# A single-token decode block on one core: every third cache pair of the main loop is loaded from ScalarE's queue instead of SyncE's

## The chip, the cores and the metric

The kernel runs on one core of one Trainium2 chip. The core's engines each follow their own instruction stream: TensorE (PE) multiplies matrices, VectorE (DVE) and ScalarE (ACT) work element by element, GpSimd (POOL) does little here, and SyncE (SP) mostly issues transfers. Transfers between the chip's memory (HBM) and the core's on-chip memory (SBUF) are carried out by 16 DMA engines; an engine that issues a transfer puts it on a queue of its own. Engines wait for each other through semaphores. The metric is the device time of one execution in microseconds (us), smaller is better.

## What is computed

Two batch rows of 512 numbers pass through a block: layer norm, attention of one new token against a cache of 8192 positions with 32 heads of 128, an output projection, a residual; then layer norm, a dense layer to 1792, squared ReLU, a dense layer back to 512, a residual. Cut to what matters:

```python
q = (layernorm(x) @ wq)                       # x: 2 x 512, wq: 512 x 4096
scores = einsum("bhqd,bhkd->bhqk", q, k_cache) * 128 ** -0.5   # k_cache: 2 x 32 x 8192 x 128
o = einsum("bhqk,bhkd->bhqd", softmax(scores), v_cache)        # v_cache: the same shape
h = x + o @ wo                                # wo: 4096 x 512
r = maximum(layernorm(h) @ w1 + b1, 0)        # w1: 512 x 1792
return h + (r * r) @ w2 + b2                  # w2: 1792 x 512
```

All of it is 32-bit floats. The two caches hold 2 x 268 MB, and each number of them is used once.

## The kernel before, in words

**The stream.** A "pair" is one head of one batch row; there are 64. The host lays out a pair's keys and values side by side, 128 partitions (rows of SBUF) by 16384 numbers, of which the first half is keys: 8,388,608 bytes, one row of 65,536 bytes per partition. One transfer brings a pair. SBUF has room for three pairs, the three slots of `ring` (line 191); pair i goes to slot i mod 3, and below u stands for that remainder.

**Before the loop** (lines 212 to 315) SP issues `wq` into slot 2, x, and pairs 0 and 1; the queries of all heads are computed; then pair 2 is issued into slot 2, in the place of `wq` (line 307).

**The loop** handles pairs 0 to 62, three to a round. For each pair PE waits for its data (`kv_full[u]`) and for a free score buffer, and multiplies the query with the keys: 32 matrix multiplications into score buffer S[k], k = u mod 2 (line 345). DVE takes the maximum (line 351), ACT the exponentials with their sum (line 358), DVE multiplies the values with the exponentials, four instructions with a sum each, writing over the values (line 363), and copies the pair's six sums away (line 367), which signals `kv_free`. SP runs a loop of its own (line 326): it takes `kv_free`, passes it on to PE as `s_free` (a score buffer is free), and issues the next pair into the slot. PE takes two `s_free` ahead of u = 0, none ahead of u = 1 and one ahead of u = 2. So u = 0 starts only when the pair ahead of it, which used the same score buffer S[0], is done; u = 1 and u = 2 may start their matrix multiplications while DVE still works on the pair ahead.

**Each engine's order.** In the loop the order of every engine is written out by hand. DVE does all of one pair before it touches the next. ACT does one exponential per pair in the same loop as PE and DVE (line 332). The code before and after the loop goes through the class `Line`, which records operations in order and adds the waits that their tiles need.

**After the loop** SP's order is (lines 479 to 495): take `kv_free` for pair 60 and issue the keys of pair 63 into slot 0; take `kv_free` for pair 61 and issue, into slot 1, the first half of `wo`, then 7/8 of the values of pair 63 (slot 0), then more of `wo`; take `kv_free` for pair 62 and issue the rest of `wo`, the rest of the values, `w1` and `w2` in six pieces. PE, in the meantime, takes one `s_free` (`token`, line 462), computes the scores of pair 63 (line 499), takes another, and the kernel joins the four sub-blocks of each pair, projects with `wo`, and runs the dense layers as the weights land. The last steps are the matrix multiplications with the last piece of `w2`, a copy and the transfer of the result (line 586).

Of the kernel before, what the change touches and what calls it, by code (L numbers as in the profile page):

```python
# [4 lines left out]
AF = mybir.ActivationFunctionType  # L5
ALU = mybir.AluOpType
AX = mybir.AxisListType
ENGINE = mybir.EngineType
# [12 lines left out]
SLOTS = 3  # L21
LOOPED = 63
# [151 lines left out]
def attention_block_kernel(nc, xd, kvd, wqd, wod, w1d, w2d, out):  # L174
    def sb(name, *shape):
        return nc.alloc_sbuf_tensor(name, [P, *shape], F32).ap()

    written = nc.alloc_semaphore("written")
    line = Line(nc)
    pe, dve, act, sp = nc.tensor, nc.vector, nc.scalar, nc.sync  # L180
    kv_full = [nc.alloc_semaphore(f"kv_full{u}") for u in range(SLOTS)]
    s_full, m_full, e_full, v_done, kv_free, s_free = (
        nc.alloc_semaphore(n) for n in ("s_full", "m_full", "e_full", "v_done", "kv_free", "s_free"))


    pick = sb("pick", NQ, P)
# [5 lines left out]
    def place(u):  # L192
        return ring[:, u * ROW : (u + 1) * ROW]

    def slot(i):
        return place(i % SLOTS)

    def keys(i):
        return slot(i)[:, :HALF].rearrange("p (j c) -> p j c", j=NQ)

    def values(i):
        return slot(i)[:, HALF:].rearrange("p (e c) -> p e c", e=NH)
# [13 lines left out]
        line.load(xr[at : at + B], xd)  # L216
    for i in range(2):
        line.op("sp", lambda e, i=i: e.dma_start(slot(i), kvd[i]).then_inc(kv_full[i], 16))
    line.op("sp", lambda e: e.sem_inc(s_free, 2))


    ones_d = sb("ones_d", P)
# [10 lines left out]
    S = [nc.alloc_psum_tensor(f"s{k}", [P, NQ * BLK], F32).ap() for k in range(2)]  # L233

    def banks(k):
        return [S[k][:, n * BLK : (n + 1) * BLK] for n in range(NQ)]
# [51 lines left out]
    for k in range(2):  # L288
        for d in range(DB):
            for j in range(NQ):  # L290
                n = k * NQ + j
# [11 lines left out]
    q3 = sb("q3", SLOTS, 32)  # L303
    QR = sb("QR", BH - LOOPED, 32)
# [6 lines left out]
    NM, LS, AC = ALL[:, :, 0], ALL[:, :, 1], ALL[:, :, 2:]  # L311
    st3 = sb("st3", SLOTS, ST)

    line.op("pe", lambda e: e.wait_ge(s_free, 2), [q3, QR], [S[0], S[1]])
    line.flush()

    def take(engine, sem, n=1):
        engine.wait_ge(sem, n).then_inc(sem, -n)  # L318

    def freed():  # L320

        take(sp, kv_free)
        sp.sem_inc(s_free, 1)

    kv3 = kvd[:LOOPED].rearrange("(r u) p c -> r u p c", u=SLOTS)
    with nc.Fori(1, LOOPED // SLOTS, 1, engines=[ENGINE.SP]) as r:
        for u in range(SLOTS):
            freed()
            sp.dma_start(slot(u), kv3[bass.ds(r, 1), u].rearrange("o p c -> p (o c)")).then_inc(kv_full[u], 16)
    all3 = ALL[:, :LOOPED].rearrange("p (r u) c -> p r u c", u=SLOTS)  # L330
    qt3 = QT[:, SLOTS : SLOTS + LOOPED].rearrange("p (r u) -> p r u", u=SLOTS)
    with nc.Fori(0, LOOPED // SLOTS, 1, engines=[ENGINE.PE, ENGINE.DVE, ENGINE.Activation],
                 head_slot={ENGINE.PE: 0}) as r:
        for u in range(SLOTS):
            k = u % 2
            s, bk = S[k], banks(k)

            if u == 0:
                take(pe, s_free, 2)
            if u == 2:  # L340
                take(pe, s_free)
            take(pe, kv_full[u], 16)
            for n in range(CS // BLK):
                for j in range(NQ):
                    made = pe.matmul(bk[n][32 * j : 32 * j + 32, :], q3[:, u, :], keys(u)[:, j, n * BLK : (n + 1) * BLK],  # L345
                                     start=True, stop=True)
            made.then_inc(s_full, 1)

            nm, ls = st3[:, u, 0:1], st3[:, u, 1:2]
            take(dve, s_full)  # L350
            dve.tensor_reduce(nm, s, axis=AX.X, op=ALU.max, negate=True).then_inc(m_full, 1)  # L351
            if u == SLOTS - 1:
                nxt = qt3[:, bass.ds(r, 1)].rearrange("p o c -> p (o c)")
                dve.tensor_scalar(q3, nxt[:, :, None].to_broadcast([P, SLOTS, 32]), 1.0, None,  # L354
                                  op0=ALU.mult)

            take(act, m_full)
            act.activation(s, s, AF.Exp, bias=nm, scale=1.0, accum_out=ls).then_inc(e_full, 1)  # L358

            take(dve, e_full)  # L360
            for e in range(NH):
                v = values(u)[:, e]
                made = dve.scalar_tensor_tensor(v, v, 1.0, s, op0=ALU.mult, op1=ALU.mult,  # L363
                                                accum_out=st3[:, u, 2 + e : 3 + e])
            made.then_inc(v_done, 1)
            take(dve, v_done)
            dve.tensor_scalar(all3[:, bass.ds(r, 1), u], st3[:, u : u + 1], 1.0, None,  # L367
                              op0=ALU.mult).then_inc(kv_free, 1)


    def scores(i, k):
        s, bk = S[k], banks(k)
        for n in range(CS // BLK):
            for j in range(NQ):
                line.matmul(bk[n][32 * j : 32 * j + 32, :], QR[:, i - LOOPED, :], keys(i)[:, j, n * BLK : (n + 1) * BLK])
# [22 lines left out]
    def weigh_max(n, pn):  # L398

        a, b = g_at[n]  # L400
        pn = pn[:, : NQ * (b - a)].rearrange("p (j i) -> p j i", j=NQ)
        for j in range(NQ):
            line.matmul(pn[:, j], pick[:, j, :], NM[:, a:b])
# [45 lines left out]
    def load_half(i, half):  # L449
        cut = slice(half * HALF, (half + 1) * HALF)  # L450
        line.load(slot(i)[:, cut], kvd[i][:, cut])
# [5 lines left out]
    def load_wo(a, b):  # L457

        cut = slice(a * D, b * D + (BIAS if b == H else 0))
        line.load(ring[:, ROW:][:, cut], wod[:, cut])  # L460

    def token():

        line.op("pe", lambda e: e.wait_ge(s_free, 1).then_inc(s_free, -1))  # L464

    def free():

        line.op("sp", lambda e: e.wait_ge(kv_free, 1).then_inc(kv_free, -1))
        line.op("sp", lambda e: e.sem_inc(s_free, 1))  # L469

    last = BH - 1
    bk0, bk1 = banks(0), banks(1)
    hp, sums, y, o = bk0
# [2 lines left out]
    gl = sb("gl", B)  # L476


    free()
    load_half(last, 0)  # L480
    free()
    load_wo(0, H // 2)
    load_values(0, 7 * CS // 2)
    load_wo(H // 2, H // 2 + WO_PIECES[0])
    free()
    load_wo(H // 2 + WO_PIECES[0], H)
    load_values(7 * CS // 2, CS // 2)
    at = 0
# [6 lines left out]
        at += n  # L495


    token()
    scores(last, 1)
    token()  # L500
    weigh_max(0, y)
    maximum(last, 1)
    exponentials(last, 1)
# [10 lines left out]
    y, o = y[:, :FQ], o[:, :P]  # L514
# [108 lines left out]
```

## Time and profile before

| what | value |
|---|---|
| median of 3 runs | 1301.19 us (1300.82 to 1301.35) |
| the profiled execution's own time | 1301.16 us |
| its span, first to last instruction | 1299.8 us |
| busy: PE, DVE, ACT | 422.4, 742.9, 143.7 us |
| moved by DMA | 561.16 MB, mean 432 GB/s |
| time of the packets of the one data queue, as a share of 16 engines' span | 99.7% |
| granted TensorE clock, mean | 0.634 |

The profile is one execution. Its page gives the busy time of each engine, the span in 40 slices, the DMA queues, the chain of work that ended last, the costliest groups of instructions and the DMA issues. Other views of the same trace give the instructions in order of time (the timeline: start, duration, engine, line, operation, output and input tile, count, and in brackets the idle time of the engine before it and what ended that), the waits added up by line, and the busy time in chosen stretches (the windows). "SPq" is SP's queue of DMA issues, "PEq" and the like an engine's own sequencer: "<-PEq L318" stands for a wait on a semaphore by the helper at line 318. "L345" is line 345 of the kernel. The time from issue to landing of a transfer includes its time behind others in the queue. 1 MB is a million bytes, while the KB in the page's list of issues is 1024 bytes.

### The profile page before, as it was taken

The numbers are of one execution on the slowest core, as the hardware profiler recorded it, in microseconds if no ns is written. First come the engines' busy times: TensorE is split into PE (matmuls) and PEld (weight loads), VectorE is DVE, ScalarE is ACT, GpSimd is POOL, SyncE is SP. The second block draws the span as 40 slices with busy tenths as digits, with TensorE's granted clock in tenths as the row PEclk, the third lists the DMA queues.
The fourth block names the chain that finished last, engine by engine and source line by source line (L and its number), as shares of the span: only waits on it lengthen the run. The fifth ranks groups of instructions, "written<-read, shape, count | busy, mean of one in ns | idle before, by whom it ended". The sixth has DMA issues, their size and how long they took to land. (4 is left out here: it accounts for less than half of the span.)

```text
span 1299.8 us, 6711 instructions
## 1 busy us (share of the span) xinstructions
PE 422.4 (32%) x2418; PEld 113.7 (9%) x2418; DVE 742.9 (57%) x709; ACT 143.7 (11%) x149; POOL 0.7 (0%) x6
## 2 busy tenths in 40 slices
PE   1423233223323323313313323322323332331347
PEld 0100000000000000000000000000000000000012
DVE  1355655655665564665665565665566565657474
ACT  1110010111011011011011011011101011101111
POOL 0000000000000000000000000000000000000000
PEclk9766566666566566656566556656656656666678
DMA  9999999999999999999999999999999999999998
GB/s 420 420 450 419 450 421 442 430 426 446 422 448 421 450 422 442 430 430 442 422 450 421 448 424 448 422 450 421 436 436 421 450 422 448 424 448 422 450 412 371
DMA packets 11069, 561.16 MB, mean 432 GB/s; under 512 B 1234, under 2 KB 1332, under 8 KB 1720
## 3 DMA queue, kind: packets, MB, share of 16 engines
q1 hardware_dynamic: 11064, 561.08, 99.7%
q8 instruction: 4, 0.07, 0.0%
q14 instruction: 1, 0.01, 0.0%
HBM read 561.03 MB, written 0.05 MB: 432 GB/s over the span
## 5 line engine op out<-in xcount | busy, mean ns | idle before, releaser
L345 PE MATMUL s<-ring,q 128*32 128x512 f32 x2016 | 376.1, 914 | 831.2 <-PEq L318 831.2
L363 DVE SCALAR_TENSOR_TENSOR ring<-ring,s 128x2048 f32<-128x2048 f32 x252 | 561.5, 2285 | 143.1 <-DVEq L318 143.1
L351 DVE TENSOR_REDUCE st<-s 128x1 f32<-128x2048 f32 x63 | 144.4, 2292 | 341.9 <-DVEq L318 341.9
L358 ACT ACTIVATE s<-s,st 128x2048 f32<-128x2048 f32 x63 | 122.3, 1942 | 1083.4 <-ACTq L318 1083.4
L345 PEld LDWEIGHTS s<-ring,q 128*32 128x32 f32 x2016 | 94.5, 159 | 1112.0 <-issue 1112.0
L363 DVE DVE_READ_ACCUMULATOR ring<-ring,s 128x1 f32 x252 | 21.0, 83 | 0.0
L367 DVE TENSOR_SCALAR ALL<-st 128x6 f32 x63 | 10.8, 172 | 15.2 <-DVEq L318 15.2
L165 DVE TENSOR_REDUCE sx<-xr 2x1 f32<-2x512 f32 x1 | 0.7, 676 | 21.2 <-DMA xr<-in_xd 21.2
L358 ACT ACTIVATION_READ_ACCUMULATOR s<-s,st 128x1 f32 x63 | 12.1, 193 | 0.0
L139 PE MATMUL s<-ring,OT 128*2 128x512 f32 (+1 forms) x70 | 10.8, 689 | 3.6 <-DMA ring<-in_wod 3.0
L139 PE MATMUL s<-ident,xr 128*128 128x4 f32 x8 | 1.9, 356 | 26.0 <-DVE xr L157 26.0
L139 PE MATMUL s<-ring,xn 128*2 128x512 f32 x64 | 9.2, 742 | 0.3 <-DVE xn L150 0.3
L161 DVE SCALAR_TENSOR_TENSOR ring<-ring,s 128x2048 f32<-128x2048 f32 x3 | 6.8, 2283 | 1.4 <-DMA ring<-in_kvd 1.4
L139 PE MATMUL s<-ring,QR 128*32 128x512 f32 x32 | 5.3, 825 | 4.6 <-DMA ring<-in_kvd 4.6
L157 DVE TENSOR_SCALAR QT<-s 128x64 f32<-128x64 f32 x1 | 0.2, 225 | 10.3 <-PE s L139 10.3
L139 PE MATMUL s<-ring,xc 128*2 128x448 f32 (+1 forms) x34 | 5.6, 725 | 0.3 <-DVE xc L153 0.3
L143 ACT ACT_TABLE_LOAD x4 | 5.1, 1283 | 0.8 <-PEq L615 0.7
L354 DVE TENSOR_SCALAR q<-QT 128x96 f32 x21 | 5.1, 243 | 0.0
L139 PE MATMUL s<-ALL,pick 128*128 128x62 f32 (+1 forms) x16 | 3.4, 352 | 5.1 <-PEq L464 4.5
L139 PE MATMUL s<-ring,a 128*2 128x128 f32 x112 | 3.6, 272 | 2.5 <-DMA ring<-in_w2d 1.8
L139 PEld LDWEIGHTS s<-ident,xr 128*128 128x128 f32 x8 | 1.8, 327 | 26.0 <-DVE xr L157 26.0
L150 DVE COPY res<-s 128x128 f32<-128x128 f32 x1 | 0.3, 292 | 5.9 <-PE s L139 5.9
(86 smaller groups left out, 50.9 us busy)
## 6 DMA issues: line engine op xcount, KB each, us to landing
ring<-in_kvd SPq DMA_DIRECT2D x1, 4096.0 KB, 28.3
ring<-in_wod SPq DMA_DIRECT2D x1, 4096.0 KB, 18.1
ring<-in_kvd SPq DMA_DIRECT2D x1, 3584.0 KB, 26.3
ring<-in_w1d SPq DMA_DIRECT2D x2, 1792.0 KB, 24.8
ring<-in_wod SPq DMA_DIRECT2D x1, 2560.0 KB, 31.8
ring<-in_w2d SPq DMA_DIRECT2D x2, 1280.0 KB, 30.5
ring<-in_wod SPq DMA_DIRECT2D x1, 1568.0 KB, 18.2
ring<-in_kvd SPq DMA_DIRECT2D x63, 37.3
```

What stands on the lines that cost most here:

```text
L139: self.op("pe", lambda e: e.matmul(out, lhsT, rhs, start=start, stop=stop), [lhsT, rhs], [out])
L143: self.op("act", lambda e: e.activation(out, in_, func, bias=bias, scale=scale, accum_out=accum_out), [in_, *more], [out] + ([] if accum_o ...
L150: self.op("dve", lambda e: e.tensor_copy(out, in_), [in_], [out])
L157: self.op("dve", lambda e: e.tensor_scalar(out, in_, by, None, op0=ALU.mult), [in_, *more], [out])
L161: self.op("dve", lambda e: e.scalar_tensor_tensor(out, a, by, b, op0=op0, op1=op1, accum_out=accum_out), [a, b, *more], [out] + ([] if acc ...
L165: self.op("dve", lambda e: e.tensor_reduce(out, in_, axis=AX.X, op=op, negate=negate), [in_], [out])
L345: made = pe.matmul(bk[n][32 * j : 32 * j + 32, :], q3[:, u, :], keys(u)[:, j, n * BLK : (n + 1) * BLK], start=True, stop=True)
L351: dve.tensor_reduce(nm, s, axis=AX.X, op=ALU.max, negate=True).then_inc(m_full, 1)
L354: dve.tensor_scalar(q3, nxt[:, :, None].to_broadcast([P, SLOTS, 32]), 1.0, None, op0=ALU.mult)
L358: act.activation(s, s, AF.Exp, bias=nm, scale=1.0, accum_out=ls).then_inc(e_full, 1)
L363: made = dve.scalar_tensor_tensor(v, v, 1.0, s, op0=ALU.mult, op1=ALU.mult, accum_out=st3[:, u, 2 + e : 3 + e])
L367: dve.tensor_scalar(all3[:, bass.ds(r, 1), u], st3[:, u : u + 1], 1.0, None, op0=ALU.mult).then_inc(kv_free, 1)
```

## The change

The loads of the loop's pairs with u = 1 (pairs 4, 7, ... 61, twenty transfers) are issued by ACT, on ACT's own DMA queue. SP's loop keeps u = 0 and u = 2. The two semaphores that carried the news of a free slot are split accordingly: the copy at the end of a pair with u = 1 signals `kv_free1`, which ACT takes and passes on to PE as `s_free1`. PE, which took two `s_free` ahead of u = 0, takes one `s_free` and one `s_free1` there.

ACT leaves the common loop and gets one of its own, so that its order can hold the load: exponentials of u = 0, exponentials of u = 1, the wait for the end of the pair u = 1 and the issue of its successor, exponentials of u = 2. Its loop has one round less than PE's and DVE's; the exponentials of the last round stand behind it. After the loop all transfers are still SP's, in the same order; the second `free` takes `kv_free1`, and the first `token` takes `s_free1`.

```diff
+    def next_load(engine, sem, freed, u, r):
+        take(engine, sem)
+        engine.sem_inc(freed, 1)
+        engine.dma_start(slot(u), kv3[bass.ds(r, 1), u].rearrange("o p c -> p (o c)")).then_inc(kv_full[u], 16)
+
+    def exponentials_of(u):
+        take(act, m_full)
+        act.activation(S[u % 2], S[u % 2], AF.Exp, bias=st3[:, u, 0:1], scale=1.0,
+                       accum_out=st3[:, u, 1:2]).then_inc(e_full, 1)
+
     with nc.Fori(1, LOOPED // SLOTS, 1, engines=[ENGINE.SP]) as r:
-        for u in range(SLOTS):
-            freed()
-            sp.dma_start(slot(u), kv3[bass.ds(r, 1), u].rearrange("o p c -> p (o c)")).then_inc(kv_full[u], 16)
+        for u in (0, 2):
+            next_load(sp, kv_free, s_free, u, r)
+    with nc.Fori(1, LOOPED // SLOTS, 1, engines=[ENGINE.Activation]) as r:
+        exponentials_of(0)
+        exponentials_of(1)
+        next_load(act, kv_free1, s_free1, 1, r)
+        exponentials_of(2)
+    for u in range(SLOTS):
+        exponentials_of(u)
...
-    with nc.Fori(0, LOOPED // SLOTS, 1, engines=[ENGINE.PE, ENGINE.DVE, ENGINE.Activation],
-                 head_slot={ENGINE.PE: 0}) as r:
+    with nc.Fori(0, LOOPED // SLOTS, 1, engines=[ENGINE.PE, ENGINE.DVE], head_slot={ENGINE.PE: 0}) as r:
...
             if u == 0:
-                take(pe, s_free, 2)
+                take(pe, s_free)
+                take(pe, s_free1)
...
-            take(act, m_full)
-            act.activation(s, s, AF.Exp, bias=nm, scale=1.0, accum_out=ls).then_inc(e_full, 1)
...
-                              op0=ALU.mult).then_inc(kv_free, 1)
+                              op0=ALU.mult).then_inc(kv_free1 if u == 1 else kv_free, 1)
...
-    free()
+    free(kv_free, s_free)
     load_half(last, 0)
-    free()
+    free(kv_free1, s_free1)
     load_wo(0, H // 2)
...
-    token()
+    token(s_free1)
     scores(last, 1)
-    token()
+    token(s_free)
```

More of the change, by code (lines that the diff above doesn't have):

```diff
@@ L181, in attention_block_kernel @@
     kv_full = [nc.alloc_semaphore(f"kv_full{u}") for u in range(SLOTS)]
-    s_full, m_full, e_full, v_done, kv_free, s_free = (
-        nc.alloc_semaphore(n) for n in ("s_full", "m_full", "e_full", "v_done", "kv_free", "s_free"))
+    s_full, m_full, e_full, v_done, kv_free, kv_free1, s_free, s_free1 = (
+        nc.alloc_semaphore(n)
+        for n in ("s_full", "m_full", "e_full", "v_done", "kv_free", "kv_free1", "s_free", "s_free1"))
     pick = sb("pick", NQ, P)
@@ L218, in attention_block_kernel @@
         line.op("sp", lambda e, i=i: e.dma_start(slot(i), kvd[i]).then_inc(kv_full[i], 16))
-    line.op("sp", lambda e: e.sem_inc(s_free, 2))
+    for sem in (s_free, s_free1):
+        line.op("sp", lambda e, sem=sem: e.sem_inc(sem, 1))
     ones_d = sb("ones_d", P)
@@ L312, in attention_block_kernel @@
     st3 = sb("st3", SLOTS, ST)
-    line.op("pe", lambda e: e.wait_ge(s_free, 2), [q3, QR], [S[0], S[1]])
+    line.op("pe", lambda e: e.wait_ge(s_free, 1), [q3, QR], [S[0], S[1]])
     line.flush()
@@ L318, in take @@
         engine.wait_ge(sem, n).then_inc(sem, -n)
-    def freed():
-        take(sp, kv_free)
-        sp.sem_inc(s_free, 1)
     kv3 = kvd[:LOOPED].rearrange("(r u) p c -> r u p c", u=SLOTS)
-    with nc.Fori(1, LOOPED // SLOTS, 1, engines=[ENGINE.SP]) as r:
-        for u in range(SLOTS):
-            freed()
-            sp.dma_start(slot(u), kv3[bass.ds(r, 1), u].rearrange("o p c -> p (o c)")).then_inc(kv_full[u], 16)
+    def next_load(engine, sem, freed, u, r):
[6 more added lines that the diff above has]
+                       accum_out=st3[:, u, 1:2]).then_inc(e_full, 1)
+    with nc.Fori(1, LOOPED // SLOTS, 1, engines=[ENGINE.SP]) as r:
+        for u in (0, 2):
[7 more added lines that the diff above has]
+        exponentials_of(u)
     all3 = ALL[:, :LOOPED].rearrange("p (r u) c -> p r u c", u=SLOTS)
     qt3 = QT[:, SLOTS : SLOTS + LOOPED].rearrange("p (r u) -> p r u", u=SLOTS)
-    with nc.Fori(0, LOOPED // SLOTS, 1, engines=[ENGINE.PE, ENGINE.DVE, ENGINE.Activation],
-                 head_slot={ENGINE.PE: 0}) as r:
+    with nc.Fori(0, LOOPED // SLOTS, 1, engines=[ENGINE.PE, ENGINE.DVE], head_slot={ENGINE.PE: 0}) as r:
         for u in range(SLOTS):
@@ L347, in attention_block_kernel @@
             made.then_inc(s_full, 1)
-            nm, ls = st3[:, u, 0:1], st3[:, u, 1:2]
+            nm = st3[:, u, 0:1]
             take(dve, s_full)
@@ L460, in load_wo, with token, free @@
         line.load(ring[:, ROW:][:, cut], wod[:, cut])
[L462 to L469, printed above, removed]
+    def token(sem):
+        line.op("pe", lambda e: e.wait_ge(sem, 1).then_inc(sem, -1))
+    def free(sem, freed):
+        line.op("sp", lambda e: e.wait_ge(sem, 1).then_inc(sem, -1))
+        line.op("sp", lambda e: e.sem_inc(freed, 1))
     last = BH - 1
@@ L484, in attention_block_kernel @@
     load_wo(H // 2, H // 2 + WO_PIECES[0])
-    free()
+    free(kv_free, s_free)
     load_wo(H // 2 + WO_PIECES[0], H)
```

## The prediction, made before the changed kernel was run

> **What bounds the kernel now.** I read the page's slices and queues first, then the windows, then the timeline around two boundaries between pairs.
>
> ```profile
> span 1299.8 us, 6711 instructions
> PE 422.4 (32%) x2418; PEld 113.7 (9%) x2418; DVE 742.9 (57%) x709; ACT 143.7 (11%) x149; POOL 0.7 (0%) x6
> DMA  9999999999999999999999999999999999999998
> q1 hardware_dynamic: 11064, 561.08, 99.7%
> ```
>
> No compute engine is busy for more than 57%, while the packets of the one queue fill 99.7% of the 16 DMA engines. The windows say whether there are gaps anywhere:
>
> ```profile
> core 0: us, PE busy (x) PEld busy (x) DVE busy (x) ACT busy (x) POOL busy (x), PEclk, DMA share, GB/s
> 62.00:1203.00 1141.00, 354.22 (x1888) 88.62 (x1888) 674.88 (x610) 121.46 (x118) 0.00 (x0) 0.61 1.00 434
> 1203.00:1243.00 40.00, 12.95 (x72) 3.41 (x76) 22.77 (x20) 4.12 (x4) 0.00 (x0) 0.63 1.01 436
> 1243.00:1261.00 18.00, 8.96 (x61) 2.13 (x53) 11.83 (x12) 2.06 (x2) 0.00 (x0) 0.87 1.01 434
> 1261.00:1297.00 36.00, 27.01 (x256) 12.07 (x260) 16.75 (x37) 7.32 (x14) 0.00 (x0) 0.81 0.96 408
> ```
>
> The DMA share is 1.00 through the whole loop and on to 1261 us, at 434 GB/s. So the kernel is a stream without holes: the time is the bytes over that rate, and it can only change if the rate does, or if the engines run dry somewhere. A pair is 8.389 MB, so at 434 GB/s its data takes 19.33 us and a round of three 58.0 us.
>
> How far is it from running dry? The cycle of a slot, in the middle of the loop:
>
> ```profile
> 604.09 6.28 PE L345 MATMUL s<-ring,q 128*32 128x512 f32 x32 [13.64 <-PEq L318]
> 604.40 0.17 DVE L367 TENSOR_SCALAR ALL<-st 128x6 f32 x1 [0.24 <-DVEq L318]
> 610.55 2.29 DVE L351 TENSOR_REDUCE st<-s 128x1 f32<-128x2048 f32 x1 [5.97 <-DVEq L318]
> 612.96 1.94 ACT L358 ACTIVATE s<-s,st 128x2048 f32<-128x2048 f32 x1 [17.86 <-ACTq L318]
> 624.32 0.17 DVE L367 TENSOR_SCALAR ALL<-st 128x6 f32 x1 [0.24 <-DVEq L318]
> 624.88 6.13 PE L345 MATMUL s<-ring,q 128*32 128x512 f32 x32 [14.51 <-PEq L318]
> ...
> 1164.32 6.06 PE L345 MATMUL s<-ring,q 128*32 128x512 f32 x32 [13.80 <-PEq L318]
> 1184.34 0.17 DVE L367 TENSOR_SCALAR ALL<-st 128x6 f32 x1 [0.24 <-DVEq L318]
> 1184.81 18.51 SPq L329 DMA_DIRECT2D ring<-in_kvd  x2
> ```
>
> A pair with u = 1 lands and PE starts at 1164.32; SP issues its successor at 1184.81, 20.5 us later. Where the scores are ready, a pair occupies DVE from the maximum at 610.55 to the end of its copy at 624.49, 13.94, say 14.0 us. What a transfer costs beside its data I take from the first one, which met an empty queue:
>
> ```profile
> ring<-in_wqd SPq DMA_DIRECT2D x1, 22.0
> DMA to landing us min/median/max: 35.4/37.2/39.6
> L329 SPq DMA_DIRECT2D ring<-in_kvd x60: 332/333/343, 62.0 to 1203.0; - x60
> ```
>
> 22.0 - 19.33 = 2.7 us, ahead of the first byte and behind the last together. So from the end of one pair's data to the first byte that its successor can bring into the slot pass 20.5 + 2.7 = 23.2 us. In the loop a transfer needs 37.2 us to land, and 37.2 - 22.0 = 15.2 of these it stands in line: the stream always has a spare. The spare is smallest behind the loop:
>
> ```profile
> 1222.30 6.09 PE L345 MATMUL s<-ring,q 128*32 128x512 f32 x32 [13.76 <-PEq L318]
> 1242.34 0.17 DVE L367 TENSOR_SCALAR ALL<-st 128x6 f32 x1 [0.24 <-DVEq L318]
> 1242.66 0.34 SPq L136 DMA_DIRECT2D ring<-in_wod  x1
> 1251.14 5.32 PE L139 MATMUL s<-ring,QR 128*32 128x512 f32 x32 [4.57 <-DMA ring<-in_kvd]
> 1260.71 2.29 DVE L165 TENSOR_REDUCE ALL<-s 128x1 f32<-128x2048 f32 x1
> 1260.85 0.33 SPq L136 DMA_DIRECT2D ring<-in_wod  x1
> ```
>
> Pair 61 lands at 1222.30, is done at 1242.5, and only then may `wo` be issued into its slot, at 1242.66. What is then still under way is pair 62 and the half pair of keys of 63, which lands at 1251.14. A transfer must be issued 2.7 us ahead of that landing to follow without a hole; it is issued 8.48 us ahead. The spare is 8.48 - 2.7 = **5.8 us**.
>
> **The change, part by part.** *The bytes, the three slots and the order of consumption* stay. *Issue:* 20 of SP's issues go to ACT. SP has nothing else to do in the loop: its 0.33 us each was hidden and saves nothing. On ACT an issue with its wait and its increment is not in this trace; from below it is nothing, from above I take SP's whole way from the start of the copy to the issue, 1184.34 to 1184.81, 0.5 us. What is queued behind it on ACT is the exponential of u = 2, whose maximum starts no sooner than that copy ends and comes 2.4 us ahead of the exponential (610.55, 612.96). 2.4 us cover 0.5, so I take 0; without cover it would be 20 x 0.5 = 10 us of compute, and of stream only as far as it exceeds a spare (below). ACT's wait for the end of pair u = 1 lasts while ACT has nothing to do in any case: the next maximum is behind that end on DVE. *PE* gets a second wait ahead of u = 0, for a semaphore that was set 14 us before: between 0 and the 0.24 us that a DVE wait shows at 624.32, only on compute that has a spare; 0. *ACT's own loop* has the same exponentials: 0.
>
> *The order of the bytes* is the real term. One queue served pairs strictly one after the other. With two queues that both hold work I let each engine alternate between them, half of the rate each. No row of this trace shows two busy data queues, so this is bounded: strict order as before (cost 0) and the halves that follow. I take the halves, as nothing in 16 independent engines keeps an order across queues.
>
> Count in data time within a round, 0 being the end of the data of u = 0, y that of u = 1, z that of u = 2, and 58.0 the next round's 0. The transfer of u = 1 (ACT) can start 23.2 after its predecessor's end, at y - 58 + 23.2 = y - 34.8. That of u = 2 (SP) starts 14.0 later, at y - 20.8, as DVE does u = 2 right behind u = 1. Until 0 the ACT transfer shares with u = 0 and gets (34.8 - y)/2; from 0 to y - 20.8 it is alone and gets y - 20.8; the rest of its 19.33 comes at half rate. So y = (y - 20.8) + 2 x (19.33 - (34.8 - y)/2 - (y - 20.8)), and y = 24.7. At that moment u = 2 has half of 24.7 - 3.9 = 20.8 us, **10.4 us of data**; it ends at z = 24.7 + 8.9 = 33.6, within the 14.0 that DVE needs anyway. Then u = 0 runs alone until the ACT transfer starts at 24.7 + 23.2 = 47.9, has 14.3 by then, shares the last 5.0 and ends at 58.0: it closes. The intervals between landings go from 19.3, 19.3, 19.3 to 24.7, 8.9, 24.4. The least that ever remains when a new transfer can start is those 5.0 us, so **no hole in the loop**: cost 0, uncovered if a load came over 5 us late.
>
> *Behind the loop* all is SP's, but pair 61 has paid for 62: when it lands, 10.4 us of 62 have been fetched that formerly came later. As the engines never rested, it lands 10.4 us later than before: PE starts it at 1232.7, and `wo` is issued at 1242.66 + 10.4 = 1253.1. The half pair still lands at 1251.1, because all that precedes it is the same bytes. The hole is 10.4 - 5.8 = **4.6 us**. Nothing wins it back: everything behind it up to the last piece of `w2` is stream. Pair 62 is done 14.0 us after 61, at 1266.9 instead of 1260.7, and releases the last pieces at 1267.1; by then the queue holds `wo`, values and `wo` of 4096 + 3584 + 2560 KB, 24.2 us from 1255.7 on, so there is a spare of 10. Compute at the end is 6.2 us late, 1.6 more than the stream, and has these waits for transfers to absorb it:
>
> ```profile
> 1269.33 2.29 DVE L161 SCALAR_TENSOR_TENSOR ring<-ring,s 128x2048 f32<-128x2048 f32 x1 [1.37 <-DMA ring<-in_kvd]
> 1294.97 1.27 PE L139 MATMUL s<-ring,a 128*2 128x128 f32 x40 [1.12 <-DMA ring<-in_w2d]
> 1296.88 1.06 PE L139 MATMUL s<-ring,a 128*2 128x128 f32 x32 [0.63 <-DMA ring<-in_w2d]
> ```
>
> 1.12 + 0.63 = 1.75 cover 1.6; without them 1.6 would be added. **Sum:** 1301.16 (the profiled execution's time) + 4.6 = 1305.8. The median, 1301.19, gives the same. A row is 65,536 bytes, 8 rows per engine and pair, 19.33/8 = 2.4 us each; if an engine alternates by whole rows, y, and with it the hole, may sit up to one such step off: about 2.2 to 7.0 us, 1303.4 to 1308.2 as this case's own range.
>
> **The rivals.** *Whole transfers in turn.* If an engine finishes its share of one transfer before it turns to the other queue, then at the end of u = 1 only u = 2 waits, and at the end of u = 2 only u = 0 (the ACT load can start 23.2 - 19.3 = 3.9 us later): the old order, no hole, 1301.2, no change; in effect the change would not do what it says. For it: 8 rows are a small share to finish. Against it: nothing in the rows. The Trainium skill, "DMA: Bandwidth & Descriptors", section "Queues, rings and completion order", says that an engine takes turns between queues by packets, typically of 9 to 17 descriptors; a share of 8 rows and its signal would be one such packet, and by that the time is 1301.2. The page of the profile counts rows as packets, 65,536 bytes at most, by which the turn comes after each row; no run so far shows which.
>
> *The rate falls while two queues are served.* The place is the shared time, 20.8 + 10.1 of each 58 us, 53% of the loop. The only slower rate of a busy stretch is that of small pieces, 408 GB/s at a share of 0.96, 425 when full, 2% under 434: 0.53 x 0.02 x 1141 = 12 us at most, so up to 1318; it decides from 0.4%, 2.6 us, on. Against it: in 1243 to 1261 pieces of unlike sizes follow each other at the full 434.
>
> *The rate rises.* If a second queue fills moments between rows, the share of 1.00 hides a reserve. The best window has 436, 0.5% over 434: 0.53 x 0.005 x 1141 = 3 us less. With the hole that is 1302.8; faster than before only if pair 61 also lands in the old order, 1298.2. Against it: 434 in every window of the loop. The Trainium skill, the same page, section "Issuing engines are not separate DMA queues", says that transfers from several engines run on the same 16 DMA engines and that this saves only issue time; by that this rival is excluded, and the trace agrees as far as one queue already fills 99.7%.
>
> *ACT's load comes late in the loop.* Above the 5.0 us spare each microsecond is a hole per round, 20 us in all. From ACT's 0.5 us that is far: 1306 to 1326.
>
> **How the numbers follow.** A measurement tells about 0.2%, 2.6 us, from no change: 1298.6 to 1303.8. Hole at the end, 60% (57 slower, 3 too small to tell); whole transfers in turn, 18%, no change; the rate falls, 12%, slower; the rate rises, 7% (5 faster, 2 no change); late loads, 3%, slower. Together: faster 5%, same 23%, slower 72%. The time is the likeliest case's, 1305.8. The range goes from 1300.6, which takes in the second case, to 1310, which leaves out the upper half of the falling rate, the late loads and the truly faster: 6 + 3 + 5 = 14%.
>
> **What the changed profile would show.** A second data queue with 20 x 8.389 = 168 MB. PE's starts in a round 24.7, 8.9 and 24.4 us apart. The loop's windows still 434 GB/s: under 432 speaks for a falling rate. Pair 61 starting at about 1232.7, the first `wo` issued near 1253, and some 4.6 us with little DMA around 1251 to 1256, after which all ends that much later. Starts 19.3 us apart would mean that the queues don't share by halves, and the forecast falls; a time over 1310 would mean that the rate, or a hole in each round, is what I mis-sized.

## The result, and the profile after

The changed kernel takes 1309.2 us in the median of four runs (1308.43 to 1310.55), the kernel before 1301.01 (1300.82 to 1301.35). The ratio is 1.0064, with a 95% interval of 1.0046 to 1.0081: slower by 0.6%, 8.2 us. The forecast was slower, 1305.8 in a range of 1300.6 to 1310. The profiled execution is one of the two shortest, 1308.45 us.

From the page of the changed kernel, its span and its queues (packets, MB, share):

```profile
span 1306.8 us, 6753 instructions
q1 hardware_dynamic: 8184, 393.31, 69.6%
q10 hardware_dynamic: 2880, 167.77, 29.6%
```

The second queue is there, with the 168 MB of twenty pairs. The windows of the changed kernel (last three columns: granted clock, DMA share, GB/s):

```profile
62.00:1203.00 1141.00, 310.05 (x1888) 81.50 (x1888) 670.72 (x609) 121.46 (x118) 0.00 (x0) 0.65 1.00 434
1243.00:1261.00 18.00, 7.90 (x52) 1.92 (x44) 13.89 (x14) 3.62 (x4) 0.00 (x0) 0.72 0.67 273
```

The loop runs at the same 434 GB/s as before. The loss stands in 18 us behind it: 273 GB/s instead of 434, (434 - 273) / 434 x 18 = 6.7 us without data. Parts of two rounds of the loop and its end, from the timeline of the changed kernel (line 362 is the old 345; the rows are pairs 55, 56 and 61, 62, then SP's first `wo`, the maximum of pair 63 and the end):

```profile
1118.04 5.87 PE L362 MATMUL s<-ring,q 128*32 128x512 f32 x32 [18.12 <-PEq L320]
1125.29 3.64 PE L362 MATMUL s<-ring,q 128*32 128x512 f32 x32 [1.37 <-PEq L320]
...
1233.99 5.92 PE L362 MATMUL s<-ring,q 128*32 128x512 f32 x32 [18.12 <-PEq L320]
1241.24 3.64 PE L362 MATMUL s<-ring,q 128*32 128x512 f32 x32 [1.32 <-PEq L320]
1254.20 0.34 SPq L136 DMA_DIRECT2D ring<-in_wod  x1
1267.98 2.29 DVE L165 TENSOR_REDUCE ALL<-s 128x1 f32<-128x2048 f32 x1
1303.82 1.05 PE L139 MATMUL s<-ring,a 128*2 128x128 f32 x32 [0.45 <-DMA ring<-in_w2d]
1304.94 0.29 DVE L150 COPY res<-s 128x128 f32<-128x128 f32 x1 [4.44 <-PE s L139]
```

From the kernel before, pair 62 and the copy of the result:

```profile
1241.60 4.97 PE L345 MATMUL s<-ring,q 128*32 128x512 f32 x32 [13.21 <-PEq L318]
1298.00 0.29 DVE L150 COPY res<-s 128x128 f32<-128x128 f32 x1 [5.92 <-PE s L139]
```

Pair 61 starts at 1233.99 instead of 1222.30, pair 62 at 1241.24 instead of 1241.60. That second number is of use throughout: pair 62 is the last of the loop to land, so its start tells how much time the stream has lost by then, whatever the order, as long as no transfer behind it is fetched along with it. Here it has lost nothing; all that is lost is lost later, because pair 61 gave up its turn. Before, `wo` was issued at 1242.66 and the last matrix multiplications started at 1296.88; now at 1254.20 and 1303.82, 11.5 and 6.9 us later.

### The profile page after: what moved, and what is told of

Its sections match the earlier page's. It is cut to its first block, busy times and chain, and to the rows that moved or that the text cites. A ratio compares the mean times of both kernels' runs of the same rounds, so it can differ in the third digit from the quotient of the medians.

```text
span 1306.8 us, 6753 instructions
## 1 busy us (share of the span) xinstructions
PE 381.4 (29%) x2418; PEld 107.4 (8%) x2418; DVE 742.4 (57%) x709; ACT 143.7 (11%) x149; POOL 0.7 (0%) x6
## 5 line engine op out<-in xcount | busy, mean ns | idle before, releaser
L362 PE MATMUL s<-ring,q 128*32 128x512 f32 x2016 | 332.0, 818 | 873.1 <-PEq L320 873.1
L362 PEld LDWEIGHTS s<-ring,q 128*32 128x32 f32 x2016 | 87.2, 144 | 1117.1 <-issue 1117.1
L333 ACT ACTIVATION_READ_ACCUMULATOR s<-s,st 128x1 f32 x63 | 12.1, 193 | 0.0
L139 PEld LDWEIGHTS s<-ALL,pick 128*128 128x128 f32 x16 | 3.6, 327 | 9.2 <-issue 8.8
```

What stands on the lines that cost most here:

```text
L139: self.op("pe", lambda e: e.matmul(out, lhsT, rhs, start=start, stop=stop), [lhsT, rhs], [out])
L333: act.activation(S[u % 2], S[u % 2], AF.Exp, bias=st3[:, u, 0:1], scale=1.0, accum_out=st3[:, u, 1:2]).then_inc(e_full, 1)
```

## The experiments

The theory to test: the loop itself costs nothing, and pair 61's lateness costs all (A). The rival: sharing costs the stream a little each time, some 0.4 us in each of twenty transfers (B).

### Undo the last shared transfer alone

```diff
-    with nc.Fori(1, LOOPED // SLOTS, 1, engines=[ENGINE.SP]) as r:
+    LAST = LOOPED // SLOTS - 1
+    with nc.Fori(1, LAST, 1, engines=[ENGINE.SP]) as r:
         for u in (0, 2):
             next_load(sp, kv_free, s_free, u, r)
+    next_load(sp, kv_free, s_free, 0, LAST)
+    next_load(sp, kv_free1, s_free1, 1, LAST)
+    next_load(sp, kv_free, s_free, 2, LAST)
...
-    with nc.Fori(1, LOOPED // SLOTS, 1, engines=[ENGINE.Activation]) as r:
+    with nc.Fori(1, LAST, 1, engines=[ENGINE.Activation]) as r:
...
-    for u in range(SLOTS):
+    for u in (0, 1, 2, 0, 1, 2):
         exponentials_of(u)
```

> Nineteen of the twenty transfers stay on ACT's queue; only the last, pair 61, goes back to SP's, in its old place between pairs 60 and 62. Theory A (one hole at the end): pair 61 no longer shares with pair 62, lands near 1222.3 and wo is issued near 1242.7, so the hole is gone and the time is 1301 to 1302. Rival B (a cost per shared transfer): 19/20 of the cost stays, 1308 to 1309.

1301.43 us in the median of eleven runs, ratio 1.0011 (1.0002 to 1.0020). From the timeline, pairs 61 and 62, `wo`, and the end:

```profile
1221.66 5.61 PE L366 MATMUL s<-ring,q 128*32 128x512 f32 x32 [8.14 <-PEq L320]
1240.98 6.19 PE L366 MATMUL s<-ring,q 128*32 128x512 f32 x32 [13.71 <-PEq L320]
1241.72 0.33 SPq L136 DMA_DIRECT2D ring<-in_wod  x1
1296.54 1.05 PE L139 MATMUL s<-ring,a 128*2 128x128 f32 x32 [0.60 <-DMA ring<-in_w2d]
```

Nineteen of twenty shared transfers are still there, and nearly all of the cost is gone. Rival B falls. The expectation missed one thing: seven runs lie between 1300.82 and 1301.91, but four between 1303.74 and 1304.61. A second, smaller cost comes and goes.

### The changed kernel once more

> The changed kernel once more, unaltered, for the spread of its times: four runs gave 1308.4, 1308.4, 1310.0 and 1310.6. Theory A (the whole cost is one hole in the stream between the last keys of pair 63 and the first half of wo, as pair 61 shared with pair 62): the times come in steps of whole rows of a share, some 2 us apart, and the profile's hole, read from the issue of wo, is as much longer or shorter as its time. Rival B (each of the twenty shared transfers costs some 0.4 us somewhere in the loop): the spread has nothing to do with the issue of wo, which stays within 0.3 us of 1254.2.

1308.52 us in the median (1305.35 to 1309.99), ratio 1.0053 (1.0039 to 1.0066). The profiled execution, the longest of the five, has a hole that the first profile lacks. A window of this run:

```profile
100.00:160.00 60.00, 15.36 (x96) 4.13 (x96) 29.50 (x28) 6.17 (x6) 0.00 (x0) 0.64 0.94 403
```

and of the changed kernel's first profile in the same 60 us:

```profile
100.00:160.00 60.00, 15.18 (x96) 3.93 (x96) 32.46 (x30) 6.18 (x6) 0.00 (x0) 0.67 1.01 436
```

Theory A's expectation, one hole behind the loop that sets each run's time, is only half right: there is a second place, the first round. The timeline of this run there (pair 2 starts, ACT issues pair 4; pair 3 starts and is done, pair 5 starts), and pair 62 much later:

```profile
82.19 5.57 PE L362 MATMUL s<-ring,q 128*32 128x512 f32 x32 [14.32 <-PEq L320]
82.32 0.39 ACTq L328 DMA_DIRECT2D ring<-in_kvd  x1
118.48 6.20 PE L362 MATMUL s<-ring,q 128*32 128x512 f32 x32 [30.72 <-PEq L320]
138.63 0.17 DVE L381 TENSOR_SCALAR ALL<-st 128x6 f32 x1 [0.24 <-DVEq L320]
140.32 5.52 PE L362 MATMUL s<-ring,q 128*32 128x512 f32 x32 [11.65 <-PEq L320]
...
1243.25 3.64 PE L362 MATMUL s<-ring,q 128*32 128x512 f32 x32 [1.73 <-PEq L320]
```

and the changed kernel's first profile at the same steps of the first round:

```profile
82.18 4.99 PE L362 MATMUL s<-ring,q 128*32 128x512 f32 x32 [13.21 <-PEq L320]
83.42 0.39 ACTq L328 DMA_DIRECT2D ring<-in_kvd  x1
115.95 5.16 PE L362 MATMUL s<-ring,q 128*32 128x512 f32 x32 [28.79 <-PEq L320]
135.07 0.17 DVE L381 TENSOR_SCALAR ALL<-st 128x6 f32 x1 [0.24 <-DVEq L320]
140.08 5.05 PE L362 MATMUL s<-ring,q 128*32 128x512 f32 x32 [8.53 <-PEq L320]
```

ACT's issue comes 1.1 us earlier in this run, pair 3 lands 2.5 us later, about one row's 2.4 us, and is done 3.6 later. Its successor can be issued some 0.5 us behind 138.63, when pair 5, the last data under way, lands at 140.32: by the prediction's rule a hole of 139.1 - 140.3 + 2.7 = 1.5 us. In the other run 135.6 - 140.1 + 2.7 is below zero, no hole. Pair 62 starts 2.0 us later than in the first profile (1243.25 against 1241.24), and `wo` is issued 1.6 later (1255.80): as late as theory A expects of a longer run, but the delay is there before the loop ends. So at the start of sharing the stream has a spare of a row or less. What decides seems to be whether ACT's first issue comes ahead of a row's turn or behind it: in this run it stands 0.1 us behind the start of pair 2 and pair 3 starts 36.3 behind pair 2, while in the four profiles with an issue 1.2 to 1.7 behind (the first, the last transfer undone, one transfer alone, the values first) pair 3 starts 33.8 behind and there is no hole. That is one profile against four, and no run set the issue on purpose.

### One shared transfer, the first

The added lines, which take the place of the two loops of SP and ACT:

```diff
+    next_load(sp, kv_free, s_free, 0, 1)
+    next_load(sp, kv_free, s_free, 2, 1)
+    with nc.Fori(2, LOOPED // SLOTS, 1, engines=[ENGINE.SP]) as r:
+        next_load(sp, kv_free, s_free, 0, r)
+        next_load(sp, kv_free1, s_free1, 1, r)
+        next_load(sp, kv_free, s_free, 2, r)
+    exponentials_of(0)
+    exponentials_of(1)
+    next_load(act, kv_free1, s_free1, 1, 1)
+    exponentials_of(2)
+    with nc.Fori(1, LOOPED // SLOTS, 1, engines=[ENGINE.Activation]) as r:
+        for u in range(SLOTS):
+            exponentials_of(u)
```

> Only the first of the twenty transfers (pair 4) is ACT's; the other nineteen go back to SP in their old places. It bears on the spread: with nineteen on ACT and the last on SP, 7 of 11 runs gave 1300.8 to 1301.9 and 4 gave 1303.7 to 1304.6, and one profile of the unaltered change has a hole in 100 to 160 us (403 GB/s) that another has not. Theory C (that hole belongs to the start of sharing, where the spare is smallest, and happens in some runs): the same two groups, 1301 and 1303.5 to 1304.6, from a single shared transfer. Rival (it can happen in any round, with a small chance): nearly all runs at 1301.

Six of the eleven runs lie at 1300.78 to 1301.69, five at 1302.98 to 1304.73; the ratio is 1.0011 (1.0002 to 1.0020), the same as with nineteen shared transfers. So the cost that comes and goes needs no more than the first shared transfer, as theory C had it, and the eighteen that follow add nothing that can be seen. The profiled execution is of the shorter group; that the longer runs have the hole of the first round is inferred from the profile above.

### Fill the hole behind the loop

```diff
     load_half(last, 0)
+    load_values(0, 7 * CS // 2)
     free(kv_free1, s_free1)
     load_wo(0, H // 2)
-    load_values(0, 7 * CS // 2)
```

> The changed kernel, but behind the loop SP issues the 3.5 MB of values of pair 63, which go to slot 0 that is already free, ahead of its wait for pair 61 instead of behind the first half of wo. Theory A: pair 61 is as late as before, 1234, and wo is issued as late, 1254, but 8.5 us of data stand in the queue in the meantime, more than the hole's 6, so the stream doesn't stop: 1301 to 1302.5, the share of DMA in 1243 to 1261 at 1.00 instead of 0.67. Rival B (a cost per shared transfer in the loop): 1308 to 1310 as it was. If the new order itself cost something (the projection waits longer for wo), the run with one queue and this order shows it.

> The kernel before, one queue, with only the new order behind the loop (values of pair 63 ahead of the wait for pair 61). Both theories: there is no hole to fill here, so 1301 within 1 us; what it differs from the kernel before is the price of the order itself, to be taken off the run with two queues and this order.

With one queue the new order takes 1300.95 us, ratio 1.0000 (0.9991 to 1.0009): the order costs nothing. With two queues it takes 1307.36 (1303.56 to 1307.84), ratio 1.0044 (1.0030 to 1.0058), where 1301 to 1302.5 was expected. Yet the hole is filled, as the window of the two-queue run shows:

```profile
1243.00:1261.00 18.00, 8.11 (x52) 1.99 (x44) 13.53 (x12) 3.98 (x4) 0.00 (x0) 0.72 0.99 428
```

The timeline of that run says what took its place (maximum of pair 63, then the last steps):

```profile
1268.34 2.29 DVE L165 TENSOR_REDUCE ALL<-s 128x1 f32<-128x2048 f32 x1
1299.80 1.27 PE L139 MATMUL s<-ring,a 128*2 128x128 f32 x40 [0.70 <-DVE a L161]
1303.54 0.29 DVE L150 COPY res<-s 128x128 f32<-128x128 f32 x1 [3.80 <-PE s L139]
```

No step waits for a piece of `w2` any more; in the kernel before the last two pieces had a wait each, in the changed one the last. From the maximum of pair 63, which stands behind pair 62 on DVE, to the copy of the result it is 35.2 us of compute. In the kernel before that would end at 1260.71 + 35.2 = 1295.9, 2.1 us ahead of the 1298.0 at which the stream let it end. So pair 62 being done 7 us late is a limit of its own, nearly as long as the hole, and filling the one leaves the other. My expectation had priced the hole alone.

### Each of the two limits by itself, with one queue

The kernel before, with DVE held up ahead of the maximum of pair 63:

```diff
     weigh_max(0, y)
+    for _ in range(6):
+        line.fused(big, big, 1.0, big, ALU.mult, ALU.max)
     maximum(last, 1)
```

> The kernel before, one queue, with six idle instructions of 128x1024 on DVE (1.28 us each, some 7 us together) ahead of the maximum of pair 63. No transfer waits for them, so the stream is untouched; only the compute behind pair 62 is late, by about as much as in the changed kernel (1267.98 against 1260.71 there). Theory A2 (compute behind pair 62 is a second limit): from that maximum to the last copy the run with the values first took 1303.54 - 1268.34 = 35.2 us with nothing to wait for; here that would end at 1260.7 + 7 + 35.2 = 1302.9 instead of 1298.0: 1306, 4.9 late. Theory A1 (only the stream counts, the waits for transfers absorb the rest): 1301 to 1302.

and with `wo` held back until the scores of pair 63 are there:

```diff
     free()
+    token()
+    scores(last, 1)
+    line.op("sp", lambda e: e.nop(), [S[1]], [])
     load_wo(0, H // 2)
...
-    token()
-    scores(last, 1)
     token()
```

> The kernel before, one queue, but SP issues the first half of wo only when the scores of pair 63 are computed, near 1256.5 instead of 1242.66; pairs 61 and 62 are done when they always were. The stream alone gets a hole, of 1256.5 - 1251.1 + 2.7 = 8.1 us by the prediction's rule. If a hole is paid in full: 1309. If the end of the kernel had room for some of it: less.

Late compute: 1306.44 us (1304.90 to 1307.99), ratio 1.0039 (1.0025 to 1.0052). Its timeline:

```profile
1269.51 2.28 DVE L165 TENSOR_REDUCE ALL<-s 128x1 f32<-128x2048 f32 x1
1304.74 0.29 DVE L150 COPY res<-s 128x128 f32<-128x128 f32 x1 [3.80 <-PE s L139]
```

8.8 us late at the maximum, 35.2 from there to the copy as above, 6.7 late at the end: the compute has 2.1 us of room, and beyond it each microsecond is paid. Late stream: 1310.01 us (1308.13 to 1311.60), ratio 1.0068 (1.0054 to 1.0081). Its timeline:

```profile
1250.50 5.34 PE L139 MATMUL s<-ring,QR 128*32 128x512 f32 x32 [4.24 <-DMA ring<-in_kvd]
1255.97 0.34 SPq L136 DMA_DIRECT2D ring<-in_wod  x1
1305.63 1.06 PE L139 MATMUL s<-ring,a 128*2 128x128 f32 x32 [0.46 <-DMA ring<-in_w2d]
```

By the rule the hole is 1256.0 - 1250.5 + 2.7 = 8.2 us; the last matrix multiplications come 1305.63 - 1296.88 = 8.75 later. As this run's keys had landed 0.64 us sooner than the 1251.14 of before, the stream lost 9.4 us in all. A hole is paid in full, and the rule is some 1.2 us short.

### Other pairs on ACT's queue

With u = 0 and with u = 2 on ACT, the semaphores split accordingly; the core of the two edits, against the change:

```diff
-        for u in (0, 2):
+        for u in (1, 2):
...
         exponentials_of(0)
+        next_load(act, kv_free1, s_free1, 0, r)
         exponentials_of(1)
-        next_load(act, kv_free1, s_free1, 1, r)
         exponentials_of(2)
```

```diff
-        for u in (0, 2):
+        for u in (0, 1):
...
-        next_load(act, kv_free1, s_free1, 1, r)
         exponentials_of(2)
+        next_load(act, kv_free1, s_free1, 2, r)
```

> ACT's queue carries the pairs with u = 0 instead of u = 1, twenty transfers as before (3, 6, ... 60). Counting halves of the rate as in the prediction, pair 60 now lands some 10 us late (about 1213), pair 61 in its old place (1223) though it is worked on only after 60, so it is done about 5 us late (1247.5), inside the spare of 5.8, and pair 62 lands and is done on time (1262). Theory A (the cost lies behind the loop, in pairs 61 and 62 being late): 1301 to 1302, with up to 3 more in runs that have a hole at the start of sharing. Rival B (each shared transfer costs the stream some 0.4 us): 1308 to 1309 as with u = 1.

> ACT's queue carries the pairs with u = 2 (5, 8, ... 62). By the same count pair 61 is done at about 1250 to 1251, so the hole ahead of wo is only 1 to 2 us, while pair 62 lands some 7 us late and is done at about 1269.5, 8 us late. Theory A1 (the hole alone costs): 1302 to 1303. Theory A2 (what the run with the values first pointed to: the compute behind pair 62 is a second limit, about as long as the stream, so that lateness of pair 62 beyond some 2 us is paid in full): 1306 to 1307.5, with the waits for transfers of the last weights gone. Rival B (a cost per shared transfer): 1308 to 1309.

u = 0: 1305.69 us (1303.99 to 1306.95), ratio 1.0032 (1.0020 to 1.0043). u = 2: 1305.60 us (1303.84 to 1306.00), ratio 1.0033 (1.0020 to 1.0045). Both are some 3 us shorter than u = 1, which speaks against B once more, and both differ from what I expected. The timeline of u = 0, pair 62 and `wo`:

```profile
1245.46 5.62 PE L360 MATMUL s<-ring,q 128*32 128x512 f32 x32 [14.28 <-PEq L319]
1251.12 0.34 SPq L136 DMA_DIRECT2D ring<-in_wod  x1
```

and of u = 2, the same, then the scores of pair 63 and the last multiplications:

```profile
1244.95 6.20 PE L361 MATMUL s<-ring,q 128*32 128x512 f32 x32 [9.71 <-PEq L320]
1249.52 0.34 SPq L136 DMA_DIRECT2D ring<-in_wod  x1
1252.14 3.64 PE L139 MATMUL s<-ring,QR 128*32 128x512 f32 x32 [0.99 <-DMA ring<-in_kvd]
1300.70 1.06 PE L139 MATMUL s<-ring,a 128*2 128x128 f32 x32 [0.62 <-DMA ring<-in_w2d]
```

Pair 62 starts 3.9 and 3.4 us later than before. For u = 0 that much has been lost ahead of it. For u = 2 it has not: pair 62 comes on ACT's queue there, and the keys of pair 63 are fetched along with it; they land at 1252.14, 1.0 us later than before, and that is what the stream has lost by then. The windows put these losses where sharing begins, and none in the loop from 250 us on (u = 0, then u = 2):

```profile
100.00:160.00 60.00, 19.36 (x128) 5.03 (x120) 39.44 (x36) 8.23 (x8) 0.00 (x0) 0.67 0.95 402
250.00:1203.00 953.00, 278.52 (x1568) 71.09 (x1568) 563.87 (x511) 102.37 (x99) 0.00 (x0) 0.62 1.00 434
```

```profile
100.00:160.00 60.00, 17.10 (x96) 4.34 (x96) 26.89 (x25) 5.95 (x5) 0.00 (x0) 0.64 0.98 422
250.00:1203.00 953.00, 293.49 (x1592) 73.26 (x1584) 562.83 (x508) 101.53 (x99) 0.00 (x0) 0.62 1.00 434
```

For u = 0, the end of the kernel costs next to nothing (the last multiplications come 4.5 us late, 0.6 more than pair 62), as expected, and the hole at the start, expected in some runs, seems to be in all seven (none is under 1303.99). For u = 2 the last step still waits for the last weights, so the stream decides, 3.8 us late, of which 2.8 are lost behind the keys of pair 63: 1.3 of them in 1243 to 1261, at 403 GB/s instead of 434, the rest is not located. Theory A2's claim that compute would decide there fell, as pair 62 was only 3.4 us late in landing, not 7; A1's 1302 to 1303 fell too.

### A later load

ACT's load behind the exponentials of u = 2:

```diff
-        next_load(act, kv_free1, s_free1, 1, r)
         exponentials_of(2)
+        next_load(act, kv_free1, s_free1, 1, r)
```

and in a second kernel four idle instructions between the two as well:

```diff
         exponentials_of(2)
+        for _ in range(4):
+            act.activation(big, big, AF.Copy).then_inc(passed, 1)
+            take(act, passed)
         next_load(act, kv_free1, s_free1, 1, r)
```

> In ACT's loop the wait and the load stand behind the exponentials of u = 2 instead of ahead of them, so each load is issued some 4.4 us later (2.3 for the maximum, 2.1 for the exponentials). The prediction gave the loop a spare of 5.0 us for such a delay. Theory A: no hole or small ones in the loop (434 GB/s in its windows, 428 at the lowest), but pair 61 is some 4 us later again and the hole ahead of wo and the late compute grow with it: 1310 to 1318. If there is no such spare, each round loses 4.4 us: 1301 + 20 x 4.4, about 1390.

> As the run with the late load, with four more idle instructions of 128x1024 on ACT (about 1.1 us each with their wait) ahead of it, so some 9 us late in all, over the spare of 5.0. Theory: now each round loses what is over the spare, 4 us or, as the lateness itself delays the next pair, up to 7: 1301 + 19 x 4 to 7, 1380 to 1440; the loop's windows fall to 405 to 385 GB/s with holes in every round. If the loop had more room than I reckon: under 1320.

Late: 1308.01 us in the median, but from 1306.62 to 1314.99, ratio 1.0057 (1.0043 to 1.0070). Later: 1457.33 us, ratio 1.1201 (1.1180 to 1.1221). A window of the late run (its profile is of the longest execution) and its second load on ACT (the copy of u = 1, the exponentials of u = 2, the issue), then the later run's timeline (a copy of u = 1, ACT issues, and issues again a round later):

```profile
250.00:1203.00 953.00, 266.37 (x1600) 68.74 (x1600) 558.20 (x504) 100.84 (x98) 0.00 (x0) 0.63 1.00 430
```

```profile
153.98 0.17 DVE L381 TENSOR_SCALAR ALL<-st 128x6 f32 x1 [0.24 <-DVEq L320]
156.54 1.94 ACT L333 ACTIVATE s<-s,st 128x2048 f32<-128x2048 f32 x1 [11.87 <-ACTq L320]
156.86 0.35 ACTq L328 DMA_DIRECT2D ring<-in_kvd  x1
```

```profile
617.33 0.17 DVE L385 TENSOR_SCALAR ALL<-st 128x6 f32 x1 [0.24 <-DVEq L320]
626.80 0.35 ACTq L328 DMA_DIRECT2D ring<-in_kvd  x1
691.76 0.35 ACTq L328 DMA_DIRECT2D ring<-in_kvd  x1
```

The late run did not delay its loads by 4.4 us. The issue goes out 0.3 us behind the start of the exponentials, not behind their end: 2.9 us behind the copy instead of 0.5, a delay of 2.4 us, in all rounds but the first, where it is 8.4. It cost the loop (434 - 430) / 434 x 953 = 8.8 us in the profiled execution, the longest, and in the median no more than the unaltered change, below the 1310 that was expected. So this run does not test the spare of 5.0 us.

In the later run the issue comes 9.5 us behind the copy, a delay of 9.0. The round takes 691.76 - 626.80 = 65.0 us instead of 58.0: 7 us lost, the upper end of what was expected, and 7.5 in the mean of eighteen rounds, with 1457 against an expected 1380 to 1440. A spare of 5.0 and one microsecond lost for each beyond it would lose 4.0. So a delay of 2.4 us is nearly covered and one of 9.0 is far from it; the spare of 5.0 itself is not shown, and either it is smaller or what exceeds it costs nearly twice.

## Why the prediction was right or wrong

**Which way, and why: right.** The queues share by about halves, pair 61 pays for 62, `wo` waits for pair 61, and the stream has a hole there and none in the settled loop. Undoing the last shared transfer alone removes it. That the time lies inside the range was in part luck: the forecast's own case ended at 1308.2, and what lies from there to 1310 was allowed for a falling rate, which did not come.

**Halves of the rate: right in the mean.** The reckoned starts 24.7, 8.9 and 24.4 us apart came as two kinds of round; the quoted rounds have 7.25 us from u = 1 to u = 2, three rows of 2.42, and others 9.7, four rows. Whole transfers in turn are excluded: pair 3 landed 115.95 - 82.18 = 33.8 us behind pair 2, neither 19.3 nor 38.7. Steps of whole rows speak for a turn after each row of 65,536 bytes. The Trainium skill, "DMA: Bandwidth & Descriptors", section "Queues, rings and completion order", lets an engine finish a packet of typically 9 to 17 descriptors first; the trace disagrees with that as far as it would have held a share of 8 rows together.

**The hole behind the loop: mis-sized, 4.6 us forecast, 6.9 measured** (1303.82 against 1296.88). Two terms make up the 2.3. `wo` was issued at 1254.2, not 1253.1, as the turns by rows left three rows of pair 62 to fetch when pair 61 landed (7.25 us from start to start), so that 62 had five rows, some 12.1 us of data, instead of 10.4 (1.1). And the 2.7 us between transfers, taken from the first one, is short by 1.2. In the four profiles with this hole the last matrix multiplications start 49.6 to 49.7 us behind the issue of `wo` (1254.20 to 1303.82 here, 1255.80 to 1305.36 once more, 1255.97 to 1305.63 with the late stream, 1260.69 to 1310.35 with the late load); in the kernel before they start 45.7 behind the landing of the keys (1251.14 to 1296.88). So a hole is the issue less the landing plus 3.9. The hole of 6.9 is within the case's own range of 2.2 to 7.0. Another 0.3 us lies outside the span.

**"No hole in the loop": wrong for its first round.** The step looked only at the settled round. When sharing begins, pair 3 lands late while nothing yet stands in line behind pair 5, and the spare is a row or less instead of 5.0 us. That is, as far as the profiles tell, the 2 to 3 us that some runs have and others not; the run with a single shared transfer has the same two groups. The first profile needs only the 6.9 and the 0.3: 1301.16 + 7.2 = 1308.4. The second, with the hole at the start, has its last multiplications 8.5 us later than before and the same 0.3: 1310.0. The 5.0 us that the prediction gave the settled loop are not shown either: with loads 9.0 us late a round lost 7.0 to 7.5, not 4.0.

**The compute behind pair 62: right that it is covered, mis-sized.** 1.6 us late beyond the stream were to be covered by 1.75. Compute came 1267.98 - 1260.71 = 7.3 us late and the stream 6.9, so only 0.3 were to be covered, and the measured room is 2.1: there was more to spare than forecast, because the hole was longer. The prediction did not say what follows from it: that a repair of the hole alone would win nearly nothing, which the run with the values first then showed.

**The rate: right.** 434 GB/s in the loop with one queue and with two; neither of the rivals about the rate came true. The Trainium skill, the same page, section "Issuing engines are not separate DMA queues", says that issuing from several engines saves only issue time, and the trace agrees as far as the rate stayed the same.

What stays open: one run of the nine of the changed kernel took 1305.35 us and one with the values first 1303.56; no profile is of such a run. One candidate: the last round may be of the kind with 9.7 us from pair 61 to 62, in which pair 61 lands a row sooner. The late run's profile ends in such a round (1241.37 and 1251.08); its pair 62 starts 9.5 us later than before and its last multiplications 13.5, so its hole costs 4.0, some 3 less than here, and 1305.35 is 3 less than 1308.5. Not shown. Every run with a shared transfer also has ACT's own loop, and none has that loop without a load in it; runs at 1300.8 show that the loop costs nothing by itself, but not that it has no part in the two groups. Why the hole at the start seems to be in every run with u = 0 on ACT, and only in some with u = 1, was not tried beyond the counts above.

## What to carry to other kernels

Where one queue already kept the DMA engines full, a second one added no bandwidth (434 GB/s with one and with two); it changed the order in which data arrive. Of two transfers that share, the earlier landed late, pair 61 by 11.7 us, and the later, pair 62, when it always did. Look for what waits for the earlier of the two: here a slot that the next weights needed, and the compute behind it, two limits of nearly the same length, so that mending one of them won 1 to 2 us of 8. A stream's spare should be reckoned at its start and at its end, not only in the settled loop, since those are the places where nothing else stands in line.

## What the runs showed that I had not expected

A start that differs by 1.1 us (ACT's first issue at 82.32 or 83.42) went with a landing a whole row, 2.5 us, later and with a hole of some 2 us; times that fall in two groups (1300.8 to 1301.9 and 1303.0 to 1304.7 with one or nineteen shared transfers) have that as their likeliest cause. In the late run ACT's issue of a transfer goes out 0.3 us behind the start of the exponentials ahead of it, while these run for 1.94. The settled loop did not repeat from round to round but came in two kinds, for most of the first profile in turn, with 7.25 and about 9.7 us from pair u = 1 to pair u = 2:

```profile
1057.67 5.34 PE L362 MATMUL s<-ring,q 128*32 128x512 f32 x32 [15.46 <-PEq L320]
1067.39 5.34 PE L362 MATMUL s<-ring,q 128*32 128x512 f32 x32 [4.37 <-PEq L320]
```

These are pairs 52 and 53 of the changed kernel, 9.72 us apart, where pairs 55 and 56 of the next round are 7.25 apart.
